# A three-stage attention and expert kernel: less work on GpSimd in its last stage, merged logits, new rules and numbers for its scheduler

## The chip, the cores and the metric

The kernel runs on one core of a Trainium2 chip. A core has five engines with queues of their own: TensorE (PE, matmuls, with weight loads shown apart as PEld), VectorE (DVE), ScalarE (ACT), GpSimd (POOL) and SyncE (SP), which here issues nearly all transfers. The metric is device microseconds (us) of one execution, the median of several. One execution was also profiled; its trace gives every instruction's start and length.

## The reference

Float32 throughout: 4 batches, 768 tokens, 8 heads of 48 channels (384 wide).

```
# stage 1: a recurrence with complex decay, per batch and head
mag = sqrt(a_re^2 + a_im^2);  scale = min(mag, 0.999) / (mag + 1e-6)
S[t] = (a[t] * scale) * S[t-1] + outer(k[t], v[t])       # S complex, 48 x 48
y[t] = q[t] @ real(S[t])
# stage 2: gated convolution, d_ff = 1024
h = relu(x @ w_in);  c = conv3(h, conv_w);  x2 = (h * sigmoid(c)) @ w_out
# stage 3: 4 experts of causal attention, head size 64, the best 2 of 4 by x2 @ w_gate
out = sum over chosen e of weight_e * softmax(mask(q_e k_e^T / 8)) v_e @ wo_e
```

## The kernel before, in words

**No loop on the chip.** The program first writes down all its operations as a list (`S.op(...)`), then a scheduler in plain Python (`Sched.run`) replays the list on a model of the engines and fixes one static order for each engine. Each operation names the engines that can do it with a price in us for each (`alts`), the tiles it reads and writes, and a priority (lower is more urgent). The replay hands a free engine the most urgent operation that is ready, has room for its tiles, and would not be done much sooner on another engine (`slack` for that; `sp` for POOL). The result is emitted in that order; waits on the chip come from the data dependencies.

**What sets the order.** The dictionary `P` holds some hundred numbers: offsets of the priorities of each unit, block and batch (`u0..`, `v0..`, `b0..`, `c0..`), of each kind of work (`pa`, `pf`, `pp`, `ps`, `pr` in stage 1; `tf`, `dn` in stage 2; `xp`, `jq`, `jv`, `jt`, `jg`, `ja`, `jf` in stage 3), limits of buffers (`na`, `no`, `nt`, `ns`, `nx`, `nq`, `nc`), and how reluctant ACT is to change its function table. The prices are the functions `act`, `acts`, `dve`, `pool` of the number of columns. `LAT` is the delay after an engine's operation before another can start on its result; a transfer is priced as 0.65 us, bytes at 360 KB/us, and 1.1 us.

**Ports and banks in the model.** DVE and POOL are kept apart by `lock`: an operation that can run on POOL, or on DVE without PSUM among its tiles, takes a common port; `alone=True` exempts one.

**Stage 1** (`s1_ops`) works on 12 units of 256 tokens. `e_ops` turns the decay into running products: logarithms and exponentials on ACT, products on DVE or POOL, prefix sums on PE against a triangle (`cum`, L437), sines and cosines, then six products that rotate k and q and transfers that regroup them by head. `m_ops` takes each of 24 chunks of 128 tokens through scores (L585), mask (L587), transposed keys (L597), the state's update (L605 to L614) and the output (L623, L627). Until stage 2 has started, gaps of PE are filled with matmuls on zeros (`heat`, L641, and `warmth`, L645).

**Stage 2** (`s2_ops`) takes 8 blocks of 384 tokens through 8 slices of d_ff: up projection (L762), relu, three taps, tanh gate (L773 to L787), down projection (L800). Matmuls run on pairs of a rounded high part and a rest. `split` makes the pair of a weight: `weights` decodes it (L684 to L694, with a maximum at L688), a copy makes the high part, a subtraction the rest. The helpers are `cp` (copy; `CPY` is ACT, DVE or POOL) and `mul` (L394, any two-input product, sum or difference, on the engines it is given). So L394 is the line of much different work.

**Stage 3** (`s3_ops`) takes 4 batches through q and k projections (`project`, L913), values and gate logits in one matmul (L863), a gate on 24 numbers per partition (`gate1`, `gate2`), and for each pair of heads and each group of three row blocks: scores (L1004), a pass on DVE that masks and takes the extreme (L1013), exp on ACT (L1016), transposes (L1030), attention times values (L962), the gate's weights spread (L944, L951), and the output projection (`final`, L983). The matmul's 260 columns are split: 256 values copied out to a tile for each block (`cp`, ACT or DVE), 4 logits copied by DVE into `lg` (L869).

Of the kernel before, what the change touches and what calls it, by code (L numbers as in the profile page):

```python
# [15 lines left out]
OP = mybir.AluOpType  # L16
# [78 lines left out]
class Sched:  # L95
    LAT = {"PE": 0.32, "ACT": 0.2, "DVE": 0.2, "POOL": 0.22, "SP": 0.05}
# [249 lines left out]
def pool(n):  # L346
    return 0.1 + n * 0.0019
# [56 lines left out]
def s1_ops(c):  # L404
# [10 lines left out]
    def e_ops(u):  # L415
# [23 lines left out]
        def polar(z, a, b):  # L439
# [16 lines left out]
                r=ks(im), w=ks(tmp), prio=pa, alone=True))  # L456
# [4 lines left out]
            S.op({"ACT": acts(N)}, lambda e: A.activation(g(tmp), g(re), AF.Exp, bias=c.cs["b_eps"], scale=-1.0),  # L461
# [14 lines left out]
        def phase(z, a, b):  # L476
# [44 lines left out]
            S.op({"ACT": acts(N)}, lambda e: A.activation(f(n), f(n), AF.Sin, scale=-TWO_PI, bias=c.cs["b_half"]),  # L521
# [46 lines left out]
    def m_ops(j):  # L568
# [60 lines left out]
        S.op({"PE": 2.07 if cc else 1.0}, f, r=[v, qp] + sm + ([s0] if cc else []), w=[ps], prio=d - P["py"])  # L629
# [41 lines left out]
def weights(c, src, cols, prio, early=False):  # L671
# [5 lines left out]
    else:  # L677
# [10 lines left out]
        S.op({"DVE": dve(cols, True), "POOL": pool(cols)}, lambda e: c.E[e].tensor_scalar(  # L688
# [127 lines left out]
def s3_ops(c):  # L816
# [14 lines left out]
    def batch(b):  # L831
# [3 lines left out]
        for tt in range(2):  # L835
# [8 lines left out]
                  ("DVE", "POOL"), "sub")  # L844
# [7 lines left out]
        v = [S.tile([128, NE], tag="v3", bufs=12) for _ in range(NCB)]  # L852
        lg = S.tile([128, NCB, E], tag="lg", bufs=2)
        for i in range(NCB):
# [13 lines left out]
            c.cp(lambda i=i: v[i].ap, lambda ps=ps: ps[:, :NE], NE, [ps], [v[i]], pz)  # L868
            S.op({"DVE": 0.07}, lambda e, ps=ps, i=i: V.tensor_copy(lg[:, i, :], ps[:, NE:]), r=[ps], w=[(lg, (i,))], prio=pz)  # L869
# [378 lines left out]
```

## Time and profile before

| | us |
|---|---|
| median of 3 runs | 676.64 (676.08 to 679.86) |
| profiled execution | 679.69 |
| its span, first to last instruction | 677.9 |
| PE busy | 640.7 (95%) |
| DVE busy | 538.7 (79%) |
| ACT busy | 458.5 (68%) |
| POOL busy | 112.4 (17%) |

The busy time of PE is that of pipelined matmuls whose ends are modelled, so a busy PE is not a PE at its peak. Idle time of an engine costs nothing unless the engine that sets the end waits for it. A group of instructions by form shows the line, engine, operation, the tiles out<-in, shapes and count, then busy us and mean ns of one, then the idle time of the engine before them and what ended it. Tiles appear by the arena that holds them (`arena_F`, `arena_R`, ...) and PSUM as `banks`.

### The profile page before, as it was taken

To read this page: it belongs to the slowest core of one execution; us is meant where nothing else is said; L and a number is where in the kernel's file an instruction comes from. 1 tells how busy PE (TensorE), PEld (TensorE's weight loads), DVE (VectorE), ACT (ScalarE), POOL (GpSimd) and SP (SyncE) were. 2 spreads that over 40 slices of the span, in tenths; PEclk is the share of its full clock that TensorE was granted. 3 is DMA by queue.
4 is the path that set the end of the run, shared out by engine and by line. 5 is a ranking of instruction groups with operands and counts; after the bars stand their busy time and mean duration, and the time that the engine had idled before them with its cause. 6 is when DMAs were issued, how large, how long until landed. Compare 5 with 4: busy or idle time off the path is not lost.

```text
span 677.9 us, 13289 instructions
## 1 busy us (share of the span) xinstructions
PE 640.7 (95%) x4852; PEld 566.5 (84%) x4852; DVE 538.7 (79%) x1193; ACT 458.5 (68%) x956; POOL 112.4 (17%) x150
## 2 busy tenths in 40 slices
PE   7899898799899999999999999998989999999994
PEld 3568597799899899999999999987887789788864
DVE  5999999989899999989748999358768645855861
ACT  7958986788898977885526657266547545755662
POOL 0733122240342411102001000002011000100100
PEclk9999998989999999999999999998999999999998
DMA  8665858746657376455033231021012001000102
GB/s 310 170 197 188 256 160 242 198 144 201 164 170 216 98 231 188 129 156 164 25 99 101 72 106 58 1 71 36 1 36 71 36 1 59 13 2 13 36 25 76
DMA packets 54605, 76.59 MB, mean 113 GB/s; under 512 B 5104, under 2 KB 45936, under 8 KB 54528
## 3 DMA queue, kind: packets, MB, share of 16 engines
q1 hardware_dynamic: 54240, 75.04, 36.1%
q8 instruction: 40, 0.66, 0.4%
q0 software_dynamic: 288, 0.59, 0.3%
q14 instruction: 37, 0.30, 0.2%
HBM read 42.51 MB, written 14.16 MB: 84 GB/s over the span
## 4 chain that ended last, share of the span: by engine, by line
PE 63%; DVE 19%; DMA 7%; ACT 6%; issue 3%; SPq 1%; POOL 0%; DVEq 0%; ACTq 0%
PE banks L800 11%; PE banks L762 9%; PE banks L913 8%; PE banks L962 6%; PE banks L1030 5%; PE banks L1004 5%; PE banks L863 4%; PE banks L983 4%; DVE arena_F L394 4%; PE banks L585 3%; DVE arena_R L394 3%; PE banks L437 2%; PE banks L623 2%; PE banks L605 2%; PE banks L627 2%
## 5 line engine op out<-in xcount | busy, mean ns | idle before, releaser
L762 PE MATMUL banks<-arena_R 128*128 128x384 f32 (+1 forms) x504 | 104.4, 342 | 1.5 <-DVE arena_Z L610 0.9
L800 PE MATMUL banks<-arena_R 128*128 128x384 f32 (+1 forms) x516 | 104.6, 344 | 0.0
L800 PEld LDWEIGHTS banks<-arena_R 128*128 128x128 f32 x516 | 89.4, 189 | 1.7 <-issue 1.3
L762 PEld LDWEIGHTS banks<-arena_R 128*128 128x128 f32 x504 | 87.8, 188 | 3.1 <-DVE arena_Z L610 1.2
L784 DVE SCALAR_TENSOR_TENSOR arena_F<-arena_F 128x386 f32<-128x386 f32 (+1 forms) x128 | 78.6, 634 | 4.0 <-ACT arena_F L781 3.0
L384 ACT ACTIVATE arena_R<-arena_F 128x384 fp32r<-128x384 f32 (+3 forms) x81 | 43.0, 542 | 56.8 <-DVE arena_F L394 23.4
L384 ACT ACTIVATE arena_F<-banks 128x256 f32<-128x256 f32 (+4 forms) x134 | 56.3, 446 | 32.1 <-PE banks L863 11.0
L1016 ACT ACTIVATE arena_F<-arena_F 128x128 f32<-128x128 f32 (+5 forms) x96 | 63.4, 663 | 15.7 <-DVE arena_F L1013 14.8
L394 DVE TENSOR_TENSOR arena_R<-arena_F,arena_R 128x384 fp32r<-128x384 f32 (+1 forms) x90 | 58.6, 666 | 16.1 <-PE banks L800 7.8
L394 POOL TENSOR_TENSOR arena_F<-arena_F 128x768 f32<-128x768 f32 x26 | 51.5, 1984 | 93.2 <-issue 23.4
L1013 DVE CUSTOM_DVE_ANT_0 arena_F<-banks,cover 128x128 f32<-128x128 f32 (+5 forms) x96 | 56.2, 618 | 10.6 <-PE banks L1004 8.6
L394 DVE TENSOR_TENSOR arena_F<-arena_F 128x768 f32<-128x768 f32 (+1 forms) x65 | 61.7, 963 | 0.6 <-ACT arena_F L451 0.5
L1030 PE MATMUL banks<-ident,arena_F 128*128 128x128 f32 x336 | 49.1, 280 | 3.8 <-DVE arena_F L1013 3.4
L358 ACT ACT_TABLE_LOAD x40 | 51.3, 1283 | 1.4 <-PEq L1240 0.8
L1030 PEld LDWEIGHTS banks<-ident,arena_F 128*128 128x128 f32 x336 | 37.4, 141 | 13.2 <-DVE arena_F L1013 4.9
L773 ACT ACTIVATE arena_F<-banks 128x384 f32<-128x384 f32 (+1 forms) x64 | 31.0, 486 | 24.6 <-PE banks L762 21.4
L394 POOL TENSOR_TENSOR arena_R<-arena_F,arena_R 128x384 fp32r<-128x384 f32 (+2 forms) x17 | 19.9, 1169 | 163.1 <-ACT arena_R L384 122.6
L386 DVE COPY arena_F<-banks 128x384 f32<-128x384 f32 (+4 forms) x86 | 42.4, 517 | 5.2 <-PE banks L951 1.6
L1004 PE MATMUL banks<-arena_R 64*128 64x384 f32 (+4 forms) x384 | 41.6, 340 | 0.2 <-DVE arena_F L1013 0.2
L925 DVE SCALAR_TENSOR_TENSOR arena_R<-banks,arena_R 128x384 fp32r<-128x384 f32 x32 | 17.8, 557 | 28.7 <-ACT arena_R L921 28.6
L962 PE MATMUL banks<-arena_F 128*64 128x384 f32 (+2 forms) x288 | 39.7, 420 | 0.3 <-ACT arena_F L384 0.3
L787 DVE SCALAR_TENSOR_TENSOR arena_F<-arena_F 128x384 f32<-128x384 f32 (+1 forms) x64 | 35.7, 580 | 3.2 <-ACT arena_F L786 2.7
(194 smaller groups left out, 1364.7 us busy)
## 6 DMA issues: line engine op xcount, KB each, us to landing
arena_F<-x_scr SPq DMA_DIRECT2D x12, 576.0 KB, 4.6
arena_Z<-v SPq DMA_DIRECT2D x12, 512.0 KB, 4.3
arena_C<-arena_F SPq DMA_DIRECT2D x36, 129.0 KB, 2.4
arena_F<-q SPq DMA_DIRECT2D x12, 384.0 KB, 4.0
arena_F<-k SPq DMA_DIRECT2D x12, 384.0 KB, 5.0
arena_B<-arena_F SPq DMA_DIRECT2D x36, 128.0 KB, 2.4
x_scr<-arena_Z SPq DMA_DIRECT2D x24, 192.0 KB, 3.2
out<-arena_F SPq DMA_DIRECT2D x24, 192.0 KB, 1.9
```

What stands on the lines that cost most here:

```text
L358: nc.scalar.preload_act_table_set(TABS[o.tab])
L384: self.A.activation(out(), in_(), AF.Copy)
L394: self.E[e].tensor_tensor(out(), a(), b(), op=self.OPS[op])
L762: PE.matmul(ps.ap, wi[f][a][:, i * 128:(i + 1) * 128], x[i].ap, start=(n == 0), stop=(n == 8))
L784: S.op({"DVE": dve(no) + 0.06}, lambda e, i=i: V.scalar_tensor_tensor(cv.ap, h[:, i:i + no], cw[:, k3 + i:k3 + i + 1], cv.ap, op0=OP.mult, ...
L800: PE.matmul(o[:, i, :], a[:, m * 128:(m + 1) * 128], g_.ap, start=(f == 0 and n == 0 and len(g) == 1), stop=(f == FT - 1 and n == 2 and i ...
L913: PE.matmul(ps.ap, wt[a][:, o:o + 128], y[:, i, :], start=(z == 0), stop=(z == 8))
L962: PE.matmul(py[64 * r:64 * r + 64, :n], v[kb][:, o:o + HD], at[r][:, kb, :n], start=(kb == 0), stop=(kb == nk - 1))
L1004: PE.matmul(ps[r][:, z, :step], a[own, qs], x[own, kk], start=(y == 0), stop=(y == 2))
L1013: S.op({"DVE": dve(n)}, lambda e, r=r, a=a, nm=nm: V.tensor_tensor_reduce(wide(a.ap), ps[r][:, :, :step], wide(c.cs["cover"][:, SEQ - n:]) ...
L1016: S.op({"ACT": acts(n) + 0.18}, lambda e, r=r, a=a, nm=nm: A.activation(a.ap, a.ap, AF.Exp, bias=nm.ap, scale=-1.0, accum_out=rs[:, at, r: ...
L1030: PE.transpose(pt[:, z, :], a[:, (g_ + z) * 128:(g_ + z + 1) * 128], ident)
```

## The change

- **POOL in stage 3.** The rests of x2 and of y (`mul` with "sub") and the copy of the gate weights (L944) can run on DVE only. In `weights` the maximum of L688 too. The copies made with `CPY` keep POOL among their engines.
- **Logits.** One tile `v` per batch holds 6 blocks of 260 columns; one copy moves values and logits, L869 is gone, and the gate reads the logits in place (`lv`).
- **Port rule.** The tensor_tensor_reduce of L454 loses `alone`. POOL's price gets a higher fixed part and an extra for 768 columns.
- **Bank rule.** An operation of an engine other than PE waits in the replay until another engine's access to the same PSUM tile has ended.
- **Transfer rule.** Latency and rate are now 1.9 us and 300 KB/us, without the added 1.1.
- **Delays.** `LAT` is shorter, and the extra before PE falls from 0.22 to 0.1 us. An operation that can only run on its producer's engine used to be ready 0.06 us after it; now at once on PE, and after `LAT` elsewhere.
- **Numbers.** Nearly all of `P` is replaced.

```diff
-P = dict(tu=22.99, lag=1.78, tf=3.56, dn=29.40, pa=28.16, pf=31.65, pp=31.74, ps=19.16, pr=13.53, kn=9.56, pd=-10.31,
...
-         tb=28.68, xp=-21.85, jq=-1.43, jp=3.08, jv=-4.00, ja=-2.43, jf=16.61, jt=5.79, ju=0.10, jw=0.26, na=13, no=2,
-         nt=6, ns=4, nx=7, nq=14, th=0.46, fr=0.20, nc=2, sd=1, ck=-587.37, up=61.76, big=0, a0=1, a1=4, u0=-0.59,
...
-         c1=-2.69, c2=1.81, c3=-0.52, pw=0.14, sp=1.00, jg=-4.92, pm=-1.39)
+P = dict(dl=1.9, db=300000, tu=23.96, lag=1.78, tf=3.235, dn=40.248, pa=24.535, pf=29.627, pp=31.544, ps=23.523,
+         pr=13.534, kn=10.259, pd=-10.126, py=-6.758, cw=9.414, cs=5.791, ne=3, sw=17.561, slack=4.735, hold=1.448,
+         wl=0.966, bl=0.603, bc=0.057, hy=15.581, tb=20.191, xp=-76.268, jq=5.455, jp=1.452, jv=-51.436, ja=4.833,
+         jf=1.255, jt=3.944, ju=-1.015, jw=0.431, na=11, no=3, nt=8, ns=5, nx=8, nq=11, th=0.327, fr=0.203, nc=3, sd=1,
+         ck=-845.704, up=-0.516, big=0, a0=1, a1=4, u0=5.537, u1=1.91, u2=-1.166, u3=-5.507, u4=-2.773, u5=4.785,
...
+         c2=15.825, c3=7.416, pw=0.401, sp=0.255, jg=-25.424, pm=2.02)
-    LAT = {"PE": 0.32, "ACT": 0.2, "DVE": 0.2, "POOL": 0.22, "SP": 0.05}
+    LAT = {"PE": 0.22, "ACT": 0.16, "DVE": 0.13, "POOL": 0.13, "SP": 0.05}
+                if e != "PE":
+                    held = max((t.busy for t in o.acc if t.reg == "P" and t.who != e), default=0.0)
+                    if held > now:
+                        later = min(later, held)
+                        continue
-                dma = max(dma, now + dur + 0.65) + o.nbytes / 360e3
-                o.end = dma + 1.1
+                dma = max(dma, now + P["dl"]) + o.nbytes / P["db"]
+                o.end = dma
+            if e != "PE":
+                for t in o.acc:
+                    if t.reg == "P":
+                        t.busy, t.who = o.end + self.LAT[e], e
-                lat = 0.06 if s.alts.keys() == {e} else self.LAT["SP" if "SP" in o.alts else e] + (0.22 if "PE" in s.alts else 0.0)
+                lat = 0.0 if e == "PE" and "PE" in s.alts else self.LAT["SP" if "SP" in o.alts else e] + (0.1 if "PE" in s.alts else 0.0)
 def pool(n):
-    return 0.1 + n * 0.0019
+    return 0.19 + n * 0.00178 + (0.28 if n == 768 else 0.0)
# stage 1, L454
-                r=ks(im), w=ks(tmp), prio=pa, alone=True))
+                r=ks(im), w=ks(tmp), prio=pa))
# weights, L688
-        S.op({"DVE": dve(cols, True), "POOL": pool(cols)}, lambda e: c.E[e].tensor_scalar(
+        S.op({"DVE": dve(cols, True)}, lambda e: V.tensor_scalar(
# stage 3
-                  ("DVE", "POOL"), "sub")
+                  ("DVE",), "sub")
-        v = [S.tile([128, NE], tag="v3", bufs=12) for _ in range(NCB)]
+        v = S.tile([128, NCB, NE + E], tag="v3", bufs=2)
+        lv = lambda: v[:, :, NE:]
-            c.cp(lambda i=i: v[i].ap, lambda ps=ps: ps[:, :NE], NE, [ps], [v[i]], pz)
-            S.op({"DVE": 0.07}, lambda e, ps=ps, i=i: V.tensor_copy(lg[:, i, :], ps[:, NE:]), r=[ps], w=[(lg, (i,))], prio=pz)
+            c.cp(lambda i=i: v[:, i, :], lambda ps=ps: ps.ap, NE + E, [ps], [(v, (i,))], pz)
-        S.op({"DVE": 2.4}, gate1, w=[lg, c4, cnt, cn2, m1], prio=d + 2)
+        S.op({"DVE": 2.1}, gate1, r=[v], w=[lg, c4, cnt, cn2, m1], prio=d + 2)
-        S.op({"DVE": 0.3, "POOL": 0.5}, lambda e: (V if e == "DVE" else G).tensor_copy(
+        S.op({"DVE": 0.3}, lambda e: V.tensor_copy(gx.ap, gs[:, :, :, None].to_broadcast([128, 3, 2, HD])), r=[gs], w=[gx], prio=d + P["jg"])
-        c.mul(lambda: yl.ap, lambda: yf.ap, lambda: yh.ap.bitcast(F32), 384, [yf, yh], [yl], d + P["ja"], ("DVE", "POOL"), "sub")
+        c.mul(lambda: yl.ap, lambda: yf.ap, lambda: yh.ap.bitcast(F32), 384, [yf, yh], [yl], d + P["ja"], ("DVE",), "sub")
```

## Rows read from the trace of the kernel before

**Rows 1.** Windows: busy us (instructions) of PE, PEld, DVE, ACT, POOL; clock, DMA, GB/s.

```profile
34.00:142.00 108.00, 95.95 (x813) 82.20 (x813) 102.35 (x192) 82.38 (x152) 29.14 (x26) 0.95 0.70 214
142.00:340.00 198.00, 193.28 (x1639) 185.06 (x1638) 182.63 (x316) 159.90 (x294) 43.14 (x58) 1.00 0.51 151
340.00:442.00 102.00, 101.94 (x612) 100.90 (x611) 77.65 (x148) 54.03 (x110) 5.72 (x27) 1.00 0.23 72
442.00:663.00 221.00, 216.81 (x1622) 177.32 (x1621) 147.92 (x462) 129.85 (x346) 20.55 (x22) 0.99 0.09 31
```

**Rows 2.** The same windows, heating matmuls of L641 alone, sum.

```profile
sum 678.00, PE 33.23 PEld 13.29; mean PE 5.54 PEld 2.21
```

**Rows 3.** The page's chain that ended last, by line, shares of the span.

```profile
PE banks L800 11%; PE banks L762 9%; PE banks L913 8%; PE banks L962 6%; PE banks L1030 5%; PE banks L1004 5%; PE banks L863 4%; PE banks L983 4%; DVE arena_F L394 4%; PE banks L585 3%; DVE arena_R L394 3%; PE banks L437 2%; PE banks L623 2%; PE banks L605 2%; PE banks L627 2%
```

**Rows 4.** Waits of PE: waiting line, releaser: us in total, times, longest.

```profile
PE banks L1030 <- DVE arena_F L1013: 3.4, 2, 1.9
PE banks L645 <- DVE arena_Z L587: 3.1, 1, 3.1
PE banks L597 <- ACT arena_Z L599: 3.0, 3, 2.0
PE banks L597 <- DMA arena_A<-arena_F: 2.8, 2, 1.8
...
PE banks L597 <- DMA arena_C<-arena_F: 1.4, 1, 1.4
```

**Rows 5.** Timeline at 456 and 505 us: start, length, engine, line, operation.

```profile
456.40 2.23 POOL L394 TENSOR_TENSOR arena_R<-arena_F,arena_R 128x1152 fp32r<-128x1152 f32 x1 [34.91 <-DVE arena_F L881]
456.65 2.01 DVE L883 TENSOR_TENSOR arena_F<-arena_F 128x24 f32<-128x24 f32 x1
...
504.97 2.62 POOL L394 TENSOR_TENSOR arena_Z<-arena_F,arena_R 128x1152 fp32r<-128x1152 f32 x1 [14.17 <-ACT arena_R L384]
505.02 2.60 DVE L886 TENSOR_TENSOR arena_F<-arena_F 128x24 f32<-128x24 f32 x1
```

**Rows 6.** Windows with a low granted clock (columns as in rows 1).

```profile
460.00:463.00 3.00, 3.00 (x11) 3.00 (x12) 2.86 (x12) 3.00 (x9) 0.00 (x0) 0.50 0.65 197
...
134.00:139.00 5.00, 5.00 (x27) 4.66 (x25) 3.58 (x9) 3.46 (x9) 0.29 (x1) 0.50 1.07 349
```

**Rows 7.** POOL by form from 442 us: count, busy us, mean ns, idle before.

```profile
L394 POOL TENSOR_TENSOR arena_R<-arena_F,arena_R 128x384 fp32r<-128x384 f32 x11 | 11.0, 1002 | 102.0 <-ACT arena_R L384 101.8
L944 POOL COPY arena_F<-arena_F 128x384 f32<-128x384 f32 x6 | 3.0, 504 | 48.2 <-ACT arena_F L1016 31.4 <-ACT arena_R L921 7.3 <-ACT arena_F L384 5.4
```

**Rows 8.** DVE by form from 442 us.

```profile
L1013 DVE CUSTOM_DVE_ANT_0 arena_F<-banks,cover 128x768 f32<-128x768 f32 x16 | 14.8, 955 | 5.7 <-PE banks L1004 5.1 <-issue 0.6
...
L869 DVE COPY arena_F<-banks 128x4 f32<-128x4 f32 x24 | 3.9, 161 | 15.0 <-ACT arena_F L384 15.0
...
L394 DVE TENSOR_TENSOR arena_R<-arena_F,arena_R 128x384 fp32r<-128x384 f32 x5 | 2.8, 558 | 0.8 <-ACT arena_R L384 0.7
...
L394 DVE TENSOR_TENSOR arena_R<-arena_F,arena_B 128x1152 fp32r<-128x1152 f32 x1 | 1.3, 1349 | 0.0
```

**Rows 9.** All engines by form, whole span.

```profile
L1016 ACT ACTIVATE arena_F<-arena_F 128x768 f32<-128x768 f32 x16 | 14.9, 930 | 9.5 <-DVE arena_F L1013 9.4
...
L459 DVE SCALAR_TENSOR_TENSOR arena_F<-arena_F 128x768 f32<-128x768 f32 x11 | 10.4, 950 | 0.0
...
L688 POOL TENSOR_SCALAR arena_F<-arena_F 128x384 f32<-128x384 f32 x5 | 10.4, 2081 | 20.6 <-ACT arena_F L684 20.6
...
L688 DVE TENSOR_SCALAR arena_F<-arena_F 128x384 f32<-128x384 f32 x11 | 3.9, 353 | 1.0 <-ACT arena_F L684 0.9
```

**Rows 10.** DVE by form up to 442 us.

```profile
L394 DVE TENSOR_TENSOR arena_F<-arena_F 128x768 f32<-128x768 f32 x51 | 54.1, 1071 | 0.5 <-ACT arena_F L451 0.5
...
L394 DVE TENSOR_TENSOR arena_R<-arena_F,arena_R 128x384 fp32r<-128x384 f32 x53 | 35.7, 685 | 8.3 <-PE banks L800 6.9 <-issue 1.3
```

**Rows 11.** DMA issues: queue, count, KB each, median us to landing.

```profile
arena_C<-arena_F SPq DMA_DIRECT2D x36, 129.0 KB, 2.4
```

More of the change, by code (lines that the diff above doesn't have):

```diff
@@ L64, in __init__ @@
         self.until = 0.0
+        self.busy, self.who = 0.0, None
         self.reg = None
@@ L460, in polar @@
                 g(re), g(tmp), 0.5, g(re), op0=OP.mult, op1=OP.add), r=ks(tmp), w=ks(re), prio=pa)
-            S.op({"ACT": acts(N)}, lambda e: A.activation(g(tmp), g(re), AF.Exp, bias=c.cs["b_eps"], scale=-1.0),
+            S.op({"ACT": acts(N) + 0.09}, lambda e: A.activation(g(tmp), g(re), AF.Exp, bias=c.cs["b_eps"], scale=-1.0),
                  r=ks(re), w=ks(tmp), prio=pa, tab="EX", grp=u)
@@ L520, in phase @@
             S.op({"ACT": acts(N), "DVE": dve(N, True)}, mag, r=ks(w), w=ks(n), prio=pp_)
-            S.op({"ACT": acts(N)}, lambda e: A.activation(f(n), f(n), AF.Sin, scale=-TWO_PI, bias=c.cs["b_half"]),
+            S.op({"ACT": acts(N) + 0.09}, lambda e: A.activation(f(n), f(n), AF.Sin, scale=-TWO_PI, bias=c.cs["b_half"]),
                  w=ks(n), prio=psn, tab="TU", grp=u)
@@ L628, in f @@
                                   start=False, stop=True)
-        S.op({"PE": 2.07 if cc else 1.0}, f, r=[v, qp] + sm + ([s0] if cc else []), w=[ps], prio=d - P["py"])
+        S.op({"PE": 1.9 if cc else 1.0}, f, r=[v, qp] + sm + ([s0] if cc else []), w=[ps], prio=d - P["py"])
         if ci == 0:
@@ L875, in gate1 @@
         def gate1(e):
-            ot = lg[:, :, None, :].to_broadcast([128, NCB, E, E])
-            me = lg[:, :, :, None].to_broadcast([128, NCB, E, E])
+            ot = lv()[:, :, None, :].to_broadcast([128, NCB, E, E])
+            me = lv()[:, :, :, None].to_broadcast([128, NCB, E, E])
             V.tensor_tensor(c4.ap, ot, me, op=OP.is_gt)
@@ L884, in gate1 @@
             V.tensor_scalar(cnt.ap, cnt.ap, 1.5, None, op0=OP.is_lt)
-            V.tensor_reduce(m1.ap, lg.ap, axis=AX.X, op=OP.max)
-            V.tensor_sub(lg.ap, lg.ap, m1[:, :, None].to_broadcast([128, NCB, E]))
-        S.op({"DVE": 2.4}, gate1, w=[lg, c4, cnt, cn2, m1], prio=d + 2)
+            V.tensor_reduce(m1.ap, lv(), axis=AX.X, op=OP.max)
+            V.tensor_sub(lg.ap, lv(), m1[:, :, None].to_broadcast([128, NCB, E]))
+        S.op({"DVE": 2.1}, gate1, r=[v], w=[lg, c4, cnt, cn2, m1], prio=d + 2)
         S.op({"ACT": 0.15}, lambda e: A.activation(lg.ap, lg.ap, AF.Exp), w=[lg], prio=d + 2, tab="EX")
@@ L961, in av @@
                     o = (2 * pr + r) * HD
-                    PE.matmul(py[64 * r:64 * r + 64, :n], v[kb][:, o:o + HD], at[r][:, kb, :n],
+                    PE.matmul(py[64 * r:64 * r + 64, :n], v[:, kb, o:o + HD], at[r][:, kb, :n],
                               start=(kb == 0), stop=(kb == nk - 1))
-        S.op({"PE": 0.66 * (nk - 2) + 0.69}, av, r=at + v[:nk], w=[py], prio=d + P["ja"])
+        S.op({"PE": 0.65 * (nk - 2) + 0.78}, av, r=at + [(v, (kb,)) for kb in range(nk)], w=[py], prio=d + P["ja"])
         yh, yl = S.tile([128, 384], F32R, tag="y3", bufs=10), S.tile([128, 384], F32R, tag="y3", bufs=10)
```

8 lines of the change are left out of this document (3 added, 5 removed).

## The prediction

> **What bounds the kernel now.** I read the engines' busy times by stretch first, then the chain that ended last, TensorE's (PE's) own list of waits, and last the forms of VectorE (DVE) and GpSimd (POOL), because the change is about those two.
>
> PE is busy nearly always, so the end is set by what it has to do and by what it stands still for. The stretches differ [rows 1]. From 34 to 142 us PE and DVE are both near full (95.95 and 102.35 of 108 us), and part of PE's time is heating: matmuls on zeros at L641, 33.23 us over the run [rows 2]. From 142 to 340 us PE has 193.28 of 198 us and DVE 182.63: both engines bind. From 340 to 442 us PE is full and nothing but PE counts. From 442 us on (attention) PE has 216.81 of 221 us and DVE only 147.92, 67%. So a microsecond of DVE is worth something before 340 us and almost nothing after it, unless PE stands behind it at that moment.
>
> The chain of work that ended last [rows 3] agrees: PE's lines lead it, and of DVE's the helper `mul` at L394 carries 4% (into F) and 3% (into R) of the span. PE's waits [rows 4] are few and can be named. The largest of the attention is the transposes of L1030, twice behind the score passes of L1013, 3.4 us in all. Before 340 us the rows show the heat of L645 behind L587 (3.1), the key transposes of L597 behind a copy (3.0) and behind transfers (2.8 and 1.4).
>
> Why L1013 was late both times is in the timeline [rows 5]. At 456.65 a 24-element product on DVE (L883) took 2.01 us and at 505.02 its neighbour L886 took 2.60 us, where the other calls of those lines are a fraction of that. Each began while a 1152-wide subtraction ran on POOL (2.23 and 2.62 us) and ended with it. So DVE and POOL shut each other out for a whole instruction when both read SBUF twice. The Trainium skill, page "SBUF — State Buffer", section "Who interferes with whom", says this too: a DVE instruction with two SBUF inputs contends with a GpSimd instruction that reads SBUF, and whoever issues second blocks.
>
> After the first of the two stops PE's granted clock falls: from 460 to 463 us it is 0.50 [rows 6], 1.2 GHz in place of 2.4, after 1.5 us without a matmul. Three microseconds at half speed cost 1.5 us of work.
>
> **The change part by part.**
>
> *Stage 3 without POOL subtractions and gate copies.* Removed from POOL after 442 us: the two 1152-wide subtractions [rows 5], eleven 384-wide ones of 1.00 us and six copies L944 of 0.50 us [rows 7]. The gain: the waits of 3.4 us and the 1.5 us at low clock, 4.9 us. The price is on DVE: 2 x 1.35 for the wide ones and 11 x 0.56 [rows 8], 6 x 0.35 for the copies, taken from L688, which is as wide and as fast a form [rows 9], 11.0 us. DVE has 73 us free in this stretch [rows 1], which is the cover; without it the price would be 11.0 us less the 3.9 us of the next paragraph, 7.1 us, and this part a loss of 2.2 us. I take -4.9, with -4.9 and +2.2 as ends. POOL isn't quite empty afterwards: copies made through `CPY` may still go there.
>
> A rule of the skill that speaks against this part is in the same section: a DVE instruction with at most one SBUF input, outside the two-port modes, doesn't contend. L1013 has one (the other operand is in PSUM). By it the small subtractions on POOL would have cost DVE nothing beside L1013, and moving them would only add their 0.56 us each, so that the sum would be up to 6.2 us later.
>
> *Logits with the values.* The copy of four logits (L869) goes: 24 x 161 ns, 3.9 us, and 15.0 us in which DVE stood at it until ScalarE (ACT) had read the same bank [rows 8]. The copy of the values is four columns wider, which is nothing to speak of. No wait of PE [rows 4] leads to it, so zero for the end, with no loss in sight: the bank comes free one short copy earlier.
>
> *Port rule of the scheduler.* New times for POOL (1.84 us for 768 columns by `pool`, 1.56 before) and the lock on L454 are meant for the collisions in stages 1 and 2. There `mul` takes 1071 ns for 768 columns x51 and 685 ns for 384 x53 [rows 10], where the hardly disturbed rows of the same length are 950 ns (L459) [rows 9] and 558 ns [rows 8]: 51 x 0.121 + 53 x 0.127 = 12.9 us of DVE lost to POOL. On the chain L394 has 7% of 677.9 us, some 46 us [rows 3]; 12.9 of the 89.8 us of these two forms is 14%, so 6.6 us of the chain. The 768-wide products may still go to POOL, so the collisions get fewer and don't vanish: half, -3.3 us. Ends: 0, and -12.9 if DVE binds all the way.
>
> *Transfer and bank rules.* A 129 KB move was reckoned at 0.65 + 0.36 + 1.1 = 2.1 us and lands in 2.4 [rows 11]; now it is 1.9 + 0.43 = 2.3. PE's waits of 2.8 and 1.4 us on such moves [rows 4] are where this can pay: half of 4.2, -2.1, ends 0 and -4.2. The rule that ACT and DVE don't touch a bank together describes what the 15.0 us show; it changes the order alone, zero.
>
> *The maximum of the weights (L688) to DVE only.* Five at 2.08 us leave POOL, five at 0.35 us come to DVE [rows 9] in a stretch where it is full: 1.8 us, ends 0 and +1.8. POOL's version also held up DVE's own products, so I take half, +0.9.
>
> *The refitted priorities.* About a hundred numbers; their effect can't be summed from rows. The two early waits that are pure order (3.1 and 3.0 us) and the low clock after the second, 5 us at half speed from 134 us [rows 6], so 2.5 us of work, bound the gain at 8.6 us; one more stop of the first kind with a low clock as at 460 us (3.1 + 1.5) bounds the loss at +4.6. I take zero.
>
> **Sum.** -4.9 - 3.3 - 2.1 + 0.9 = -9.4 us. The profiled execution took 679.69 us (span 677.9), so 670.3; the median of the runs shown, 676.64, lies 3.05 us below it, so 667.2, and I say 667.
>
> **Rivals.**
>
> *DVE binds stages 1 and 2 outright.* Then the lost 12.9 us come back whole, 9.6 us more than I take: 658. For it: 285 of 306 us busy from 34 to 340 us [rows 1]. Against it: PE is as full from 142 us on, so what DVE gains there PE must be able to use.
>
> *The time goes back into DVE's queue.* The eleven microseconds of subtractions stand ahead of L1013 where POOL's stood, PE's waits at the batch changes stay, and the collisions of stage 1 only move. Left are -2.1 + 0.9: 675. For it: the queue is in order and the wide subtraction is still 1.35 us. Against it: the blocked products were 2.0 and 2.6 us long, and DVE is a third idle.
>
> *Fewer query and key tiles (slower).* The limit on `qk` tiles falls from 14 to 11 and the priority of the projections goes back. A batch takes eight, so beside a running batch three of the next can exist where there were six; its projections, PE's filler while a row group's softmax runs, come later. If PE then has nothing at a batch's start, it waits for one pass of L1013 and L1016, 0.955 + 0.930 us [rows 8, 9], and 1.5 us of clock as at 460 us: 3.4 us a stop. Each of the three batch changes has two pairs of heads, six places. At four stops it decides (667 + 13.6 = 681), at six it is 688. Against it: after the first pair of heads four tiles come free, and the value projections, now far ahead, can fill.
>
> The skill's "Perfetto Trace Analysis", section "Optimizing Scalar/DVE Operations", says that work may leave a saturated DVE even for GPSIMD, though the shared port may eat the gain; with L688 the change goes the other way. By that rule its 1.8 us would count in full, and the sum would be 0.9 us later.
>
> **Chances.** The forecast 0.60 (by itself 661 to 673), DVE binding outright 0.14, time given back 0.14, missing tiles 0.12. A timing of this kernel can tell about 0.5% (3.4 us) from no change: 673.3 and 680.0 are the bounds. The forecast's upper edge gives 0.04 to no change, so faster 0.70, same 0.18, slower 0.12. The range: all the terms at their lower ends would give 646, at their upper ends 685; down to 653 it holds most of the second case, up to 682 the third and the start of the fourth.
>
> **What would show it.** Right: no POOL subtraction after 442 us, L883 and L886 at their short times, the 3.4 us of L1030 gone, granted clock 1.00 at the start of attention; `mul` nearer 950 and 558 ns; PE's waits on L597's transfers halved. Wrong: PE waits on L1013 as before with a DVE subtraction ahead of it; idle PE at the batch changes with L913 just behind; or the first 142 us, whose order the new numbers set afresh, longer than now.

## The result and the profile after

| | us | |
|---|---|---|
| kernel before, beside it | 678.25 | 676.08 to 680.62, 4 runs |
| changed kernel | 657.18 | 654.43 to 665.44, 4 runs |
| ratio | 0.9675 | 95% interval 0.9606 to 0.9744 |

So 21 us faster, inside the range of 653 to 682 and 10 us below the 667 forecast. The ratio leaves out the execution of 665.44 us, so it lies a little under that of the two medians (0.969). The first profile of the changed kernel fell on its longest execution, 665.44 us, with two stretches of TensorE at half its clock; the rows of after below are therefore those of a second profile of the same program, 658.26 us. The mean granted clocks, first profile and second:

```profile
core 0: 663.6 us, clock 0.985
```

```profile
core 0: 656.5 us, clock 0.998
```

The rest of this section is the second profile. Its page, busy time by engine and the chain that ended last by line:

```profile
PE 631.7 (96%) x4857; PEld 562.9 (86%) x4866; DVE 532.5 (81%) x1215; ACT 467.9 (71%) x962; POOL 35.1 (5%) x103
...
PE banks L811 8%; PE banks L773 8%; PE banks L924 8%; PE banks L1040 6%; PE banks L972 6%; PE banks L1014 6%; DVE arena_F L405 5%; PE banks L875 4%; PE banks L993 4%; PE banks L596 3%; DVE arena_F L795 2%; PE banks L616 2%; DVE arena_R L405 2%; ACT L369 2%; DVE arena_Z L598 2%
```

Lines are some 10 higher than in the kernel before: L811 is its L800 (down projection), L924 its L913, L405 its L394 (`mul`), L1040 its L1030. POOL fell from 112.4 to 35.1 us, yet DVE did not rise: 538.7 before, 532.5 now. PE still leads the chain [rows 3] and `mul` still has its 7%.

Windows by stretch (columns as in [rows 1]; the third now ends at 425, where stage 2 does):

```profile
34.00:142.00 108.00, 99.81 (x868) 84.67 (x874) 103.14 (x200) 80.77 (x146) 8.56 (x17) 1.00 0.72 212
142.00:340.00 198.00, 196.50 (x1667) 188.49 (x1666) 186.07 (x344) 169.08 (x306) 14.54 (x45) 1.00 0.56 160
340.00:425.00 85.00, 85.00 (x487) 84.89 (x484) 71.21 (x137) 51.16 (x102) 3.06 (x22) 1.00 0.28 87
425.00:656.50 231.50, 223.70 (x1691) 188.69 (x1689) 144.77 (x458) 138.81 (x357) 2.58 (x5) 0.99 0.09 32
```

The waits of PE, which answer [rows 4] (waiting line, releaser: us in total, times, longest), without two groups of 0.2 us:

```profile
PE banks L448 <- ACT arena_F L492: 5.7, 5, 2.2
PE banks L448 <- DVE arena_F L474: 1.8, 5, 0.8
PE banks L652 <- DVE lt L1065: 1.6, 1, 1.6
PE banks L608 <- DMA arena_A<-arena_F: 1.5, 1, 1.5
PE banks L596 <- DMA arena_B<-arena_F: 1.5, 1, 1.5
PE banks L656 <- ACT arena_Z L644: 1.4, 1, 1.4
PE banks L448 <- ACT arena_F L784: 0.8, 1, 0.8
PE banks L608 <- DMA arena_D<-arena_F: 0.6, 1, 0.6
PE banks L608 <- ACT arena_F L509: 0.6, 1, 0.6
PE banks L608 <- DMA arena_B<-arena_F: 0.3, 1, 0.3
```

Stage 3 has disappeared from this list: after 425 us PE waits for no other engine. All that is left waits at lines of stage 1 and its heat. The largest group, prefix sums behind ACT's work on the decay, was the largest before as well, which [rows 4] doesn't show; it has not shrunk:

```profile
PE banks L437 <- ACT arena_F L481: 4.1, 3, 2.1
```

POOL's only form after 425 us and DVE's two largest `mul` forms before it, which answer [rows 7] and [rows 10]:

```profile
L399 POOL TENSOR_SCALAR arena_R<-arena_F 128x384 fp32r<-128x384 f32 x5 | 2.6, 516 | 225.1 <-ACT arena_F L395 163.4 <-DVE arena_F L405 61.7
```

```profile
L405 DVE TENSOR_TENSOR arena_F<-arena_F 128x768 f32<-128x768 f32 x77 | 72.9, 961 | 0.9 <-DMA arena_F<-q 0.7
...
L405 DVE TENSOR_TENSOR arena_R<-arena_F,arena_R 128x384 fp32r<-128x384 f32 x51 | 27.4, 551 | 5.6 <-ACT arena_R L395 5.6
```

The products now run at 961 and 551 ns, against 1071 and 685, and all 77 of 768 columns run on DVE, 26 more than before.

**Where the 21 us are.** I split each span into four. The waits are the sum of PE's list. The low clock is the span times (1 - mean granted clock), the time that the slow stretches lack to full speed. The heat is the busy time of the two lines of matmuls on zeros, in a window over the whole span. The rest is mainly what PE has to do, with the start and the end of the run. The kernels of the last five rows are those of the experiments.

| profile | span | waits | low clock | heat | rest |
|---|---|---|---|---|---|
| before | 677.9 | 28.2 | 10.2 | 35.2 | 604.3 |
| after, first profile | 663.6 | 15.3 | 10.0 | 37.8 | 600.5 |
| after, second profile | 656.5 | 16.2 | 1.3 | 35.8 | 603.2 |
| old numbers in the changed kernel | 683.2 | 22.7 | 11.6 | 42.9 | 606.0 |
| new numbers in the kernel before | 728.7 | 45.9 | 24.8 | 52.1 | 605.9 |
| changed kernel, old rules | 701.3 | 34.4 | 14.0 | 49.6 | 603.3 |
| before, offsets rounded | 694.4 | 36.2 | 13.2 | 36.8 | 608.2 |
| after, offsets rounded | 659.4 | 14.4 | 2.0 | 36.8 | 606.2 |

Over spans from 656 to 729 us the rest stays between 600 and 608 (in the other six profiles, between 601 and 610): the orders differ mainly in the waits, the clock that falls after them, and the heat that fills gaps. Differences of a few us of one row to another are too small for this split: the two profiles of the same program differ by 2.7 in the rest. From before to the second profile the waits give 12.0 us, the low clock 8.9 and the rest 1.1, together 22, less 0.6 more heat: the 21.4 us of the span. Of the 12.0 us, 4.1 are the four groups of stage 3 in the list of before, led by the 3.4 us of L1030 [rows 4]; the other 8 are stages 1 and 2.

The clock's share is too large here, for two reasons. Of the low clock, 3.2 us before and 1.6 now fall behind the last matmul, where PE has nothing left to do. And the second profile is the execution with the highest clock: over the 47 executions of the kernel before that the experiments timed, the mean clock is 0.987, and over the five of the changed kernel 0.993, by the same sum 8.8 and 4.9 us. So of the 21 us some 4 are the clock's as a rule, and some 17 would be there at full clock too.

Stage by stage this is harder to read, because the order moved work across the border. The last down projection starts at 442.6 us before and at 425.5 now. But the windows up to it, q and k projections alone (busy us of PE and PEld, then clock, DMA, GB/s), show 54 of those matmuls ahead of it before and 18 now, 7.0 us that only went to the other side. Before:

```profile
0.00:442.60 442.60, 10.51 (x54) 9.66 (x55) 0.99 0.51 155
```

and after:

```profile
0.00:425.50 425.50, 3.47 (x18) 3.21 (x19) 1.00 0.55 162
```

### The profile page after: what moved, and what is told of

Its sections match the earlier page's. It is cut to its first block, busy times and chain, and to the rows that moved or that the text cites. A ratio compares the mean times of both kernels' runs of the same rounds, so it can differ in the third digit from the quotient of the medians.

```text
span 663.6 us, 13253 instructions
## 1 busy us (share of the span) xinstructions
PE 640.1 (96%) x4866; PEld 571.0 (86%) x4866; DVE 531.6 (80%) x1215; ACT 468.4 (71%) x962; POOL 33.3 (5%) x103
## 4 chain that ended last, share of the span: by engine, by line
PE 59%; DVE 17%; DMA 6%; ACT 6%; issue 3%; SPq 1%; DVEq 0%; ACTq 0%
PE banks L811 9%; PE banks L924 8%; PE banks L773 8%; PE banks L1040 6%; PE banks L972 6%; PE banks L1014 6%; DVE arena_F L405 5%; PE banks L875 4%; PE banks L993 3%; PE banks L596 3%; DVE arena_F L795 2%; PE banks L616 2%; DVE arena_R L405 2%; PE banks L634 1%; DVE arena_Z L598 1%
## 5 line engine op out<-in xcount | busy, mean ns | idle before, releaser
L811 PE MATMUL banks<-arena_R 128*128 128x384 f32 (+1 forms) x468 | 92.2, 345 | 0.0
L395 ACT ACTIVATE arena_F<-banks 128x384 f32<-128x384 f32 (+5 forms) x144 | 61.5, 479 | 38.3 <-PE banks L875 10.2
L811 PEld LDWEIGHTS banks<-arena_R 128*128 128x128 f32 x468 | 82.3, 191 | 0.4 <-issue 0.4
L405 DVE TENSOR_TENSOR arena_F<-arena_F 128x768 f32<-128x768 f32 (+1 forms) x91 | 79.4, 892 | 1.2 <-DMA arena_F<-q 0.4
L795 DVE SCALAR_TENSOR_TENSOR arena_F<-arena_F 128x384 f32<-128x384 f32 (+1 forms) x128 | 75.4, 618 | 2.7 <-ACT arena_F L792 2.3
L395 ACT ACTIVATE arena_R<-arena_F 128x384 fp32r<-128x384 f32 (+3 forms) x82 | 44.9, 564 | 37.3 <-DVE arena_F L405 15.9
L405 DVE TENSOR_TENSOR arena_R<-arena_F,arena_R 128x384 fp32r<-128x384 f32 (+2 forms) x99 | 56.1, 581 | 11.4 <-ACT arena_R L395 10.2
L397 DVE COPY arena_F<-banks 128x384 f32<-128x384 f32 (+5 forms) x76 | 34.2, 473 | 26.0 <-PE banks L1040 16.3
L1040 PE MATMUL banks<-ident,arena_F 128*128 128x128 f32 x336 | 44.3, 277 | 0.0
L784 ACT ACTIVATE arena_F<-banks 128x384 f32<-128x384 f32 (+1 forms) x64 | 30.9, 488 | 14.6 <-PE banks L773 13.4
L797 ACT ACTIVATE arena_F<-arena_F 128x384 f32<-128x384 f32 (+1 forms) x64 | 32.3, 521 | 12.1 <-DVE arena_F L795 11.6
L1040 PEld LDWEIGHTS banks<-ident,arena_F 128*128 128x128 f32 x336 | 36.9, 141 | 4.5 <-DVE arena_F L1023 1.4
L598 DVE TENSOR_TENSOR arena_Z<-banks,tri 128x512 f32<-128x512 f32 x48 | 31.9, 683 | 9.0 <-PE banks L596 9.0
L652 PE MATMUL banks<-cover 128*128 128x512 bf16 x148 | 36.7, 394 | 1.6 <-DVE lt L1065 1.6
L634 PE MATMUL banks<-arena_Z 128*64 128x128 f32 x384 | 36.7, 280 | 0.0
L972 PEld LDWEIGHTS banks<-arena_F 128*64 128x64 f32 x288 | 19.2, 136 | 19.1 <-issue 16.0
```

What stands on the lines that cost most here:

```text
L395: self.A.activation(out(), in_(), AF.Copy)
L405: self.E[e].tensor_tensor(out(), a(), b(), op=self.OPS[op])
L634: PE.matmul(ps[64 * i:64 * i + 64, g_, :], v[:, ci, 2 * g_ + i, :], sm[g_ // 2][:, 2 * (g_ % 2) + i, :], start=True, stop=(cc == 0))
L795: S.op({"DVE": dve(no) + 0.06}, lambda e, i=i: V.scalar_tensor_tensor(cv.ap, h[:, i:i + no], cw[:, k3 + i:k3 + i + 1], cv.ap, op0=OP.mult, ...
L811: PE.matmul(o[:, i, :], a[:, m * 128:(m + 1) * 128], g_.ap, start=(f == 0 and n == 0 and len(g) == 1), stop=(f == FT - 1 and n == 2 and i ...
L972: PE.matmul(py[64 * r:64 * r + 64, :n], v[:, kb, o:o + HD], at[r][:, kb, :n], start=(kb == 0), stop=(kb == nk - 1))
```

## The experiments

**The changed kernel once more**, unchanged, for a profile without the two slow stretches.

> The changed kernel once more, for a second trace. Its other executions took 654 to 659 us, the profiled one 665.4: expected 653 to 660 us, with the span shorter by about the time in which the first trace shows a low granted clock before 142 us (0.93 and 0.96), some 5 to 7 us.

658.26 us, clock 0.998 over the span, which is 7.1 us shorter than in the first profile; the low clock alone is 8.7 us less, the waits 0.9 more.

**Stage 3 alone.** The kernel before with its order as it is; the POOL subtractions and gate copies of stage 3 are issued to DVE.

```diff
-        o.fn(o.eng)
+        o.fn("DVE" if o.eng == "POOL" and o.name == 3 and "ACT" not in o.alts and "DVE" in o.alts else o.eng)
```

> The kernel before with its order kept as it is; only the subtractions and the gate copies that stage 3 gives to POOL (two 1152 wide, some eleven 384 wide, six copies) run on DVE at the same places of the order. Theory (POOL's wide subtractions shut DVE out and PE stands behind it): the 3.4 us of PE's waits and 1.5 us at low clock go, -4.9 us, ratio about 0.993, and L883 and L886 are 0.2 us long. Rival (the time goes back into DVE's queue): within 0.3% of no change, PE waits on L1013 behind a DVE subtraction.

677.43 us (12 runs) against 680.21 (23 runs). The medians differ by 2.8 us; the ratio with its interval, which isn't that of the medians, is 0.9988 [0.9952, 1.0024], so -0.8 us [-3.3, +1.6], no change that can be told. Its trace does most of what the prediction said. DVE's timeline (start and length; L886 and L889 are L883 and L886 of before, L395 the wide subtraction):

```profile
457.26 0.18 DVE L886 TENSOR_TENSOR arena_F<-arena_F 128x24 f32<-128x24 f32 x1
...
457.77 0.18 DVE L889 TENSOR_TENSOR arena_F<-arena_F 128x24 f32<-128x24 f32 x1
...
458.50 1.35 DVE L395 TENSOR_TENSOR arena_R<-arena_F,arena_R 128x1152 fp32r<-128x1152 f32 x1
```

Its window after the batch change has the clock at 1.00, where before had 0.50 [rows 6]:

```profile
460.00:465.00 5.00, 4.71 (x33) 3.73 (x33) 4.83 (x17) 4.06 (x10) 0.61 (x1) 1.00 0.33 118
```

and of the 3.4 us of the transposes behind the score pass one group is left in PE's waits from 425 us, while the scores now wait there:

```profile
PE banks L1007 <- DVE arena_F L1016: 0.7, 2, 0.5
...
PE banks L1033 <- DVE arena_F L1016: 0.2, 1, 0.2
```

PE's waits in this stage fall from 4.1 to 2.5 us in all: a part of them moved to other lines. The 11 us of work that came to DVE raised its busy time by 3.6 us only (538.7 to 542.3), in part because its own instructions are 5.1 us shorter with no subtraction of POOL beside them. Stage 3, from the last down projection to the end, took 232.0 us against 235.3. So 3 us come back in this stage of the profiled execution, and the timing can't tell that from nothing; 4.9 lies outside its interval.

**Stages 1 and 2 alone.** The same with the POOL products, subtractions and maxima of stages 1 and 2 (`o.name in (1, 2)` in the line above).

> The kernel before with its order kept; every product, subtraction and maximum that stages 1 and 2 give to POOL runs on DVE at the same place of the order. Theory of the prediction (DVE loses 12.9 us to POOL, but POOL carries some 33 us that DVE would have to do): DVE gets about 20 us more in stretches where it is over 90% busy, slower by 10 to 18 us (ratio 1.015 to 1.026). Rival (POOL's help is worth nothing, because DVE is shut out for as long as it saves): within 0.5%, or faster.

676.73 us, ratio 0.9953 [0.9921, 0.9985]: 3.2 us faster [-5.4, -1.0], where my theory had 10 to 18 us slower. The rival was right. This is the strongest result on POOL. In the kernel before, up to 442 us, POOL had 26 products of 768 columns (51.5 us), 13 smaller ones (15.5) and five maxima (10.4), 77.4 us. At DVE's own prices that is 26 x 0.95 + 13 x 0.55 + 5 x 0.353 = 33.6 us more for DVE. The page of this run:

```profile
PE 642.3 (95%) x4844; PEld 567.9 (84%) x4852; DVE 543.2 (80%) x1237; ACT 458.7 (68%) x956; POOL 35.8 (5%) x106
```

DVE's busy time rose by 4.5 us only, from 538.7 to 543.2. Compared form by form up to 442 us (the mean before less the mean here, times the count before), DVE had been losing 24 us to POOL. 13.3 of them are in the two forms of [rows 10], so the 12.9 of my count was right for those; what it left out is `mul` of 386 columns and of 96 partitions (3.8), the taps at L784 and L787 (4.1), L454 (1.5) and others. (Busy time counts once what overlaps, so it rises by less than the 9.6 us that 33.6 and 24 leave.) The two forms at their own speed:

```profile
L395 DVE TENSOR_TENSOR arena_F<-arena_F 128x768 f32<-128x768 f32 x77 | 72.4, 950 | 2.1 <-DMA arena_F<-k 1.8 <-ACT arena_F L452 0.3
...
L395 DVE TENSOR_TENSOR arena_R<-arena_F,arena_R 128x384 fp32r<-128x384 f32 x55 | 29.6, 551 | 8.2 <-PE banks L802 6.9 <-issue 1.3
```

**POOL back, in the changed kernel.** Order as it is; the eight 1152-wide rests of x2 go to POOL, all else stays.

```diff
-        o.fn(o.eng)
+        o.fn("POOL" if o.name == "rest" else o.eng)
```

> The changed kernel with its order kept; only the eight 1152-wide subtractions of the x2 halves run on POOL at the same places. Theory (a wide POOL subtraction shuts DVE out for 2.2 to 2.6 us and PE stands behind it): each of the eight costs up to 2.5 us and at least half of them reach PE, so 5 to 13 us over the changed kernel: 662 to 670 us, ratio to the kernel before 0.976 to 0.988. Rival (DVE has a third of stage 3 free, so its hold-ups are hidden): 655 to 659 us, ratio 0.966 to 0.971.

662.4 us, 0.977 [0.9708, 0.9831]: some 4 to 5 us above the changed kernel (657 to 658), with intervals that overlap. Its timeline shows one collision in full, here with stage 2 still running (start and length; in brackets the idle time before):

```profile
353.97 2.22 POOL L406 TENSOR_TENSOR arena_Z<-arena_F,arena_Z 128x1152 fp32r<-128x1152 f32 x1 [5.29 <-ACT arena_Z L396]
353.99 3.16 DVE L797 SCALAR_TENSOR_TENSOR arena_F<-arena_F 128x386 f32<-128x386 f32 x2
...
356.65 0.53 ACT L799 ACTIVATE arena_F<-arena_F 128x386 f32<-128x386 f32 x1 [2.38 <-DVE arena_F L797]
...
357.61 1.51 PE L775 MATMUL banks<-arena_R 128*128 128x386 f32 x7 [1.04 <-ACT arena_F L786]
```

Two taps that need 1.24 us take 3.16 while POOL subtracts, ACT stands 2.38 us behind them and PE 1.04 behind ACT: a collision like those of [rows 5], made again. But the theory wanted at least half of the eight to reach PE, and that isn't what the trace shows. Four of them run after 425 us, where PE waits only once, 0.6 us, and PE's waits over the whole span are 16.3 us, as without them (16.2). The profile's span is 3.3 us longer than that of the second profile (659.8 and 656.5 us), and about as much is low clock before any of the eight has run, the first at 345.9 us:

```profile
130.00:140.00 10.00, 10.00 (x78) 9.77 (x77) 8.09 (x15) 5.55 (x8) 0.84 (x1) 0.66 0.38 130
```

So this run doesn't show that wide subtractions on POOL cost the changed kernel anything.

**POOL allowed in stage 3 of the changed kernel**, where the scheduler decides.

```diff
-                  ("DVE",), "sub")
+                  ("DVE", "POOL"), "sub")
-        S.op({"DVE": 0.3}, lambda e: ...
+        S.op({"DVE": 0.3, "POOL": 0.5}, lambda e: ...
```

(both subtractions and the gate copy)

> The changed kernel in which the scheduler may again give stage 3's subtractions and gate copies to POOL; all else as changed. Theory of the prediction (POOL's wide subtractions cost some 4.9 us): 659 to 664 us, ratio 0.973 to 0.98, if at least two wide ones go there and PE waits for L1023 behind them. Rival (with the new port prices few go there, or they are hidden): 654 to 659 us, ratio 0.966 to 0.972.

660.27 us, 0.9714 [0.9666, 0.9762], not to be told from the changed kernel. From 420 us on POOL takes five 384-wide subtractions and seven gate copies and no wide one, so the theory's condition was not met. With the new prices and numbers the ban costs and brings little; what wide subtractions would cost, this run can't say.

**The last POOL work of stages 1 and 2 in the changed kernel on DVE** (the edit of the second experiment, on the changed kernel).

> The changed kernel with its order kept; the products, subtractions and such that stages 1 and 2 still give to POOL run on DVE at the same places. If POOL's help is worth nothing, as the same edit of the kernel before showed (ratio 0.9953): 650 to 657 us, 0.2 to 0.7% under the changed kernel. Rival (under the new port rule POOL only gets what DVE has no time for): slower by 2 to 6 us, 659 to 664 us.

659.18 us, 0.9734 [0.9689, 0.9778]: no gain, where I had expected 650 to 657 us; nor is it clearly slower. POOL's busy time goes from 35.1 to 18.8 us, DVE's from 532.5 to 536.0. The new order probably had little left that collides.

**Logits apart.** The changed kernel with six tiles of values and the copy of four logits back.

```diff
-            c.cp(lambda i=i: v[:, i, :], lambda ps=ps: ps.ap, NE + E, [ps], [(v, (i,))], pz)
+            c.cp(lambda i=i: v[i].ap, lambda ps=ps: ps[:, :NE], NE, [ps], [v[i]], pz)
+            S.op({"DVE": 0.07}, lambda e, ps=ps, i=i: V.tensor_copy(lg[:, i, :], ps[:, NE:]), r=[ps], w=[(lg, (i,))], prio=pz)
```

> The changed kernel with the logits copied apart again by DVE (24 copies) into a tile of their own and the values in six tiles, all else as changed, the order replayed. Theory of the prediction (no wait of PE leads to that copy): 654 to 660 us, within 0.4% of the changed kernel. Rival (DVE's 15 us behind ACT at the bank return as waits of PE): 661 us or more.

658.41 us, 0.9709 [0.9669, 0.9748]: as the changed kernel. The 3.9 us of copies and the 15.0 us that DVE stood at them [rows 8] were worth nothing at the end that could be told.

**Old numbers.** The changed kernel, all its rules, with the priorities of before in `P` (and the new transfer price).

```diff
-P = dict(dl=1.9, db=300000, tu=23.96, ...
+P = dict(dl=1.9, db=300000, tu=22.99, ...
```

> The changed kernel with every edit and every new rule, but the numbers of the kernel before in P (and 1.9 us and 300 KB/us for transfers). Theory A (the refitted numbers are the gain, because they order stages 1 and 2 anew): most of it goes, 670 to 682 us, ratio 0.985 to 1.005. Rival B (the truer rules and prices carry it whatever the numbers): 655 to 665 us, ratio 0.965 to 0.98.

682.7 us, 1.0041 [1.001, 1.0072], or +2.8 us [+0.7, +4.9]. All the edits together, without the new numbers, are worth nothing; the numbers then bring 25.5 us. PE's longest waits are again in stage 1, behind the mask (in this kernel L597) and, as in every profile, behind ACT's work on the decay (L491):

```profile
PE banks L633 <- DVE arena_Z L597: 5.2, 4, 1.9
PE banks L447 <- ACT arena_F L491: 5.1, 2, 3.0
```

**New numbers alone**, in the kernel before.

> The kernel before with the new numbers of P and nothing else: old rules, old prices, POOL and the copies of the logits as before. Theory A: most of the gain is there, 658 to 668 us, ratio 0.97 to 0.985, PE in stages 1 and 2 some 12 us earlier done. Rival C (numbers and rules only work together, since the numbers were fitted on replays by the new rules): 672 us or more, ratio 0.99 or more. Rival B: no gain.

729.91 us, 1.076 [1.0698, 1.0821]: 52 us slower. The same numbers that bring 25 us under the new rules lose twice that under the old, as rival C said. Waits of PE:

```profile
PE banks L624 <- DVE arena_Z L588: 6.6, 4, 2.6
...
PE banks L598 <- ACT arena_Z L600: 4.2, 5, 2.1
PE banks L801 <- DVE arena_Z L395: 4.2, 1, 4.2
```

**Old rules.** The changed kernel with its numbers and its edits of stage 3, but the old delays, transfer price, POOL price and `alone`, and without the bank rule.

```diff
-    LAT = {"PE": 0.22, "ACT": 0.16, "DVE": 0.13, "POOL": 0.13, "SP": 0.05}
+    LAT = {"PE": 0.32, "ACT": 0.2, "DVE": 0.2, "POOL": 0.22, "SP": 0.05}
-                dma = max(dma, now + P["dl"]) + o.nbytes / P["db"]
-                o.end = dma
+                dma = max(dma, now + dur + 0.65) + o.nbytes / 360e3
+                o.end = dma + 1.1
-    return 0.19 + n * 0.00178 + (0.28 if n == 768 else 0.0)
+    return 0.1 + n * 0.0019
```

> The changed kernel with its edits and its numbers, but the old rules: old delays, no bank rule, old transfer price, old POOL price, L454 outside the lock. Theory A: the rules by themselves are worth little, 656 to 664 us, ratio 0.967 to 0.98. Rivals B and C: 668 us or more, ratio 0.985 or more.

703.53 us, 1.035 [1.0295, 1.0404]. Its list of waits begins with the key transposes (L603):

```profile
PE banks L603 <- ACT arena_Z L605: 5.4, 4, 3.2
PE banks L603 <- DMA arena_A<-arena_F: 4.5, 4, 2.5
...
PE banks L603 <- DMA arena_B<-arena_F: 3.5, 1, 3.5
```

On transfers they wait 8.0 us, where the changed kernel's wait 2.4. It may be that with the old price the replay believed these transfers came earlier than they do; but the delays and the bank rule went back in the same run, and the price of a 129 KB move differs by 0.2 us only.

**Offsets rounded to whole microseconds**, in before and in after: does an order hang on the decimals of its numbers?

```diff
-u0=5.537, u1=1.91, u2=-1.166
+u0=6, u1=2, u2=-1
```

> The kernel before with the same offsets rounded to whole us, nothing else. Theory F: it loses too, 684 us or more, ratio 1.007 or more. Rival R: within 0.7% of the kernel before.

> The changed kernel with the offsets of priorities in P (units, blocks, batches, kinds of work) rounded to whole us; limits of buffers, thresholds and rules as they are. Theory F (the numbers fit one replay under exactly these rules, and any small deviation loses): 665 us or more, ratio 0.98 or more, PE's waits well over 15 us. Rival R (truer rules give good orders of themselves, the numbers' last digits don't matter): within 0.7% of the changed kernel, 653 to 662 us, ratio 0.962 to 0.975.

Before: 695.7 us, 1.0246 [1.0193, 1.03], the waits up by 8.0 us. After: 662.85, 0.9784 [0.9724, 0.9843], its waits 14.4. The old order hung on its decimals; the new one loses some 1% by this, between the two theories, with intervals that overlap.

## Why the prediction was right and where it was wrong

**The failed step** is "The refitted priorities. About a hundred numbers; their effect can't be summed from rows. [...] I take zero." Everything else in my sum, -9.4 us, measured +2.8 [+0.7, +4.9] with the old numbers in place; the whole gain came with the term that I had put at nothing. Four timings, ratios to before, show that this was the change:

| | old rules | new rules |
|---|---|---|
| old numbers | 1 | 1.0041 (with all other edits) |
| new numbers | 1.076 (no other edit), 1.035 (edits of stage 3 kept) | 0.9675 |

Neither is worth anything without the other. The likely reason is that a set of priorities is fitted to the replay that turns it into an order, and under another replay it gives one that nobody looked for. The new numbers are also more than priorities: limits of buffers and thresholds changed with them (`nq` from 14 to 11, `slack` from 0.33 to 4.735), and which of them acted wasn't tried. My bounds, -8.6 to +4.6, came from two early waits and one low clock, out of 24.1 us of waits that PE had before stage 3. They didn't cover -25.5, the step from old to new numbers with all else in place. What vanished was not two waits but a few tenths to 3 us in many places, and the low clock that followed some of them. The two waits I named did shrink: L645's 3.1 us is now 1.4 (L656), L597's 3.0 behind ACT's copy has no successor in the list. The largest, which I overlooked, did not: 4.1 us of prefix sums behind ACT (L437) are now 5.7 (L448). So the early waits were the right place to look, and the zero was the wrong value.

That 657 lies in my range is largely luck. Its lower end was 653 to hold the rival in which DVE binds, and that rival didn't act (see below); by itself the forecast covered 661 to 673.

That the new rules are nearer to the chip, and the fit to them carries over for that reason, would fit the rounding and the transfer waits under old rules. It isn't shown: a longer search could have had the same effect. Nor was it tried which of the rules matters.

**Stage 3 without POOL: mechanism right, size too large.** In the changed kernel every sign came: no POOL subtraction after 425 us, the products at 0.18 us, PE's wait gone, the clock at 1.00 after the batch change. But done alone it timed at -0.8 us [-3.3, +1.6] where I had taken -4.9, with 2.5 of the 4.1 us of waits still there, at other lines in the main. Put back on POOL in the changed kernel, the wide subtractions left PE's waits as long as they were. DVE's third of idle time covered the added work, as the prediction said.

The score passes on DVE, which have one operand in PSUM, were not held up by POOL. Their min, median and max are 247, 605 and 958 ns before and 249, 604 and 958 with POOL's subtractions gone. In the trace of before, 20 of the 96 passes ran while POOL subtracted, and each took as long as the others of its width; of the 640 columns wide, 11 beside POOL and 5 alone all took 0.82 us:

```profile
481.88 0.82 DVE L1013 CUSTOM_DVE_ANT_0 arena_F<-banks,cover 128x640 f32<-128x640 f32 x1 [0.61 <-ACT arena_R L384]
481.96 1.02 POOL L394 TENSOR_TENSOR arena_R<-arena_F,arena_R 128x384 fp32r<-128x384 f32 x1 [11.30 <-ACT arena_R L384]
```

The Trainium skill, "SBUF — State Buffer", section "Who interferes with whom", says that a DVE instruction with at most one SBUF input, outside the two-port modes, doesn't contend with GpSimd. Here it agrees; the products with two SBUF inputs were held, taking up to 2.60 us in place of 0.18 [rows 5].

**Port rule: not timed by itself.** I took -3.3 us for it. Moving all of POOL's products, subtractions and maxima in stages 1 and 2 to DVE measured -3.2 us [-5.4, -1.0], but that is another edit, and the agreement is luck: with the old numbers the rule, among all the others, brought nothing. The loss behind it was 24 us and not 12.9. I had counted only the two disturbed forms of L394, and not that POOL's help saved DVE next to nothing: 77.4 us of POOL relieved DVE of 4.5 us of busy time. The Trainium skill's "Perfetto Trace Analysis", section "Optimizing Scalar/DVE Operations", warns that offloading from DVE to GpSimd might not help, because they share a port. Here the trace agrees: DVE's slower instructions ate 24 of the 33.6 us.

**Transfers: not halved.** PE's waits on regrouping transfers went from 4.2 to 1.5 + 1.5 + 0.6 + 0.3 = 3.9 us. At the key transposes alone they fell to 2.4, but the scores (L596) now wait 1.5 where they waited for no transfer. With all the old rules the new numbers wait 8.0 us at the key transposes; that the price does this was not tried by itself.

**L688 and the logits: small, as taken.** The logits measured nothing that could be told. The maxima ran on DVE in the second experiment as part of a gain, so +0.9 has no support; by itself it wasn't tried.

**Rivals.** "DVE binds stages 1 and 2 outright" gave 658, the measured time, by a mechanism that didn't act: DVE's load from 34 to 340 us did not fall, it rose from 285.0 to 289.2 us [rows 1], since products of POOL came to it, and the kernel became 21 us faster all the same. "Back into DVE's queue" is excluded by the empty list after 425 us, and so is "fewer query and key tiles": PE never stands at a batch change, although only 18 q and k matmuls now run ahead of the end of stage 2.

## What to carry to other kernels

Split a span into PE's work, its waits, the low clock and filler matmuls before guessing at causes: here the work was 600 to 610 us in all fourteen profiles, and most of every large difference was in the other three. Bound an unknown term by the whole sum of the waits and not by the two that have a name. In a statically scheduled kernel the priorities and the rules of the replay are one thing: test them crossed, and never take a refit for zero. Before counting what POOL relieves DVE of, count what DVE loses while POOL runs: if both read SBUF twice, moving all of it to DVE may cost nothing.

## What the runs showed of the hardware that was not expected

The same program at the same place does not always get the same clock. The two profiles of the changed kernel, windows just after two of the long waits (columns as above). First profile:

```profile
29.00:36.00 7.00, 6.59 (x32) 6.62 (x33) 2.67 (x7) 2.89 (x7) 1.51 (x2) 0.51 0.48 121
135.00:145.00 10.00, 10.00 (x52) 9.68 (x53) 7.43 (x15) 5.65 (x8) 0.84 (x1) 0.50 0.33 120
```

Second profile:

```profile
29.00:36.00 7.00, 6.83 (x71) 6.63 (x72) 5.69 (x15) 4.96 (x10) 1.51 (x2) 1.00 0.69 188
130.00:140.00 10.00, 9.19 (x94) 8.57 (x94) 9.50 (x19) 7.92 (x14) 0.84 (x1) 1.00 0.55 186
```

PE's timeline ahead of them (in brackets how long PE stood), first profile and then second:

```profile
29.41 0.98 PE L596 MATMUL banks<-arena_B,arena_A 96*128 96x128 f32 x3 [1.82 <-DMA arena_B<-arena_F]
...
134.08 0.38 PE L656 MATMUL banks<-cover 128*128 128x512 bf16 x1 [1.73 <-ACT arena_Z L644]
```

```profile
29.17 1.02 PE L596 MATMUL banks<-arena_B,arena_A 96*128 96x128 f32 x7 [1.52 <-DMA arena_B<-arena_F]
...
130.81 0.38 PE L656 MATMUL banks<-cover 128*128 128x512 bf16 x1 [1.39 <-ACT arena_Z L644]
```

A wait for the same transfer that was 0.3 us longer (1.82 us in place of 1.52) was followed by 7 us at a granted clock of 0.51, 1.2 GHz in place of 2.4, and so 32 matmuls in place of 71 in the same 7 us; at the second place 1.73 us were followed by 10 us at 0.50, and 1.39 us by none. So a few tenths of a microsecond of waiting go with 3 to 5 us of lost speed; the length of the stop alone doesn't settle it, since in the kernel before a stop of 1.54 us at 458 us was followed by 0.50 [rows 6] and one of 1.86 us at 506 us by 1.00:

```profile
459.87 0.90 PE L1030 MATMUL banks<-ident,arena_F 128*128 128x128 f32 x3 [1.54 <-DVE arena_F L1013]
...
508.02 0.33 PE L1030 MATMUL banks<-ident,arena_F 128*128 128x128 f32 x1 [1.86 <-DVE arena_F L1013]
```

```profile
507.00:510.00 3.00, 1.98 (x12) 1.48 (x13) 3.00 (x11) 2.26 (x9) 0.59 (x1) 1.00 0.18 51
```

Executions of one program spread by 12 us (672.79 to 684.44 over 23 of the kernel before). Differences of one profile to another below that size are no evidence without a timing.
